# Talking-heads attention with MoE and MLP: softmax scaling moved to GpSimd, a new table of copy costs

## The chip, the cores and the metric

The kernel runs on one core of a Trainium2 chip. The core has a matrix engine (PE, with its weight loads shown apart as PEld), a vector engine (DVE), an activation engine (ACT), GpSimd (POOL) and a queue that issues transfers (SP). Each works through its own list of instructions in order; a semaphore holds an instruction until what it needs is there. The metric is the device time of one launch in microseconds (us). The kernel before took 1386.21 us in the median of three runs (1384.71 to 1386.72).

## The reference

```python
scores = scale * np.matmul(q, k.transpose(0, 1, 3, 2))        # 4 x 12 heads x 448 x 448
scores = np.einsum('bhij,hg->bgij', scores, w_pre)            # heads mixed with each other
scores = scores - np.max(scores, axis=-1, keepdims=True)
attn = np.exp(scores)
attn = attn / (np.sum(attn, axis=-1, keepdims=True) + 1e-09)
attn = np.einsum('bhij,hg->bgij', attn, w_post)               # and mixed again
return np.matmul(attn, v)
```

Its rows (1792 tokens of 768) go through a mixture of eight experts, one per token, and then through an MLP `(h * cos(h)) @ w_out` with `h = x @ w_in`. All is fp32.

## The kernel before

Attention is one long loop in `attention`. The 448 query rows of a batch are cut into four chunks (120, 120, 120, 88 rows). For each chunk and head, `qk` multiplies queries and keys on PE, and the scores go from PSUM to the SBUF tile `S`. To mix heads, a *block* gathers ten query rows of all twelve heads, 120 partitions by 448 (nine rows in the last blocks): `relay` moves them by a transfer from `S` to `x`. There are 180 blocks, and per block these steps follow:

- `premix` (L193): PE multiplies `x` with the mixing matrix `kpre` into `m`; DVE takes the negated row maximum `nm`; ACT makes the exponentials `E` and, by an accumulator, their row sums `sg`.
- `scale` (L206): DVE adds 1e-9 to the sums (`rs`, L210), takes the reciprocal (L211) and multiplies the second mixing matrix `kpost` by it, row by row (`kr`, 120x120, L213). So the softmax is divided by its sums in the weights and not in the exponentials.
- `postmix` (L216), two blocks later: PE multiplies `E` with `kr` into `pa` (four matmuls), and ACT or DVE copies it to `AT`. When a chunk is complete, `av` multiplies with the values (`px`, copied to `xc`), and `rows` turns the result (`pt`, copied to `xr`) for the store.

Between the blocks stand other jobs. In the second half of a batch the keys and queries of the next are turned (`split_k`, `split_q`): ACT rounds the turned keys `tp` to `KH`, DVE takes the rest `KL`, and as each tile needs both halves of its partitions filled, GpSimd copies `KH` (L102) and DVE copies `KL` (L106; in the first batch GpSimd, L104). `narrow64` is the *side conversion*: 64 jobs bring the MLP's weights from eight-byte to four-byte numbers, each with a load `W` (two buffers), a square on ACT (L1294), four DVE operations on `f` (L1299 to L1302; the last three read two SBUF tiles) and a store. `side()` is called once per block and starts a job when its counter has reached one (64 jobs over 170 blocks).

`Balance` deals out the copies that either engine could do. It keeps an account of us for ACT (`act`) and for DVE (`dve`), has a price per copy for each (`a`, `d`), and gives the copy to the engine whose account would be lower; the code adds to the accounts by hand what goes to a fixed engine.

The order in which `attention` is written is not the order on an engine: outside of the stretches marked `manual_schedule` a scheduler of the framework places the instructions by its own costs, so a change in the code moves instructions well beyond its place. The buffers `E` (3), `m` (2), `pa` (2), `kr` (4), `sg` and `rs` (4) bound how far the engines run apart.

Behind attention, `between` and the expert stage start; their first gather, weights and routing follow attention's last blocks.

Of the kernel before, what the change touches and what calls it, by code (L numbers as in the profile page):

```python
# [11 lines left out]
F32 = mybir.dt.float32  # L12
# [6 lines left out]
ALU = mybir.AluOpType  # L19
# [12 lines left out]
class Balance:  # L32
# [4 lines left out]
        self.act = self.dve = 0.0  # L37

    def copy(self, out, in_, n):
        a, d = 0.19 + n * 0.00083, 0.07 + n * 0.00104  # L40
        if self.act + a <= self.dve + d:
            self.act += a
            return self.nc.scalar.copy(out, in_)  # L43
        self.dve += d
        return self.nc.vector.tensor_copy(out, in_)  # L45


def attention(ctx, qctx, tc, q, k, v, w_pre, w_post, wg, xs, lg, ident, nb=4, side=None, route=None):
# [3 lines left out]
    nc = tc.nc  # L52
    B, H, S, D = q.shape
# [10 lines left out]
    bal = Balance(nc)  # L64
# [29 lines left out]
    def split_k1(b, j, i, ps):  # L94

        h = 2 * j + i
        kh = ok.tile([128, S], F32R, tag=f"KH{h}", name=f"KH{b}_{h}")
        kl = ok.tile([128, S], F32R, tag=f"KL{h}", name=f"KL{b}_{h}")
        r, o = HALF[i], HALF[1 - i]
        nc.scalar.copy(kh[r], ps[r, :S])  # L100
        nc.vector.tensor_tensor(kl[r], ps[r, :S], kh[r].bitcast(F32), op=ALU.subtract)
        nc.gpsimd.tensor_scalar(kh[o], kh[r].bitcast(F32), 1.0, 0.0, op0=ALU.mult, op1=ALU.add)  # L102
        if b == 0:
            nc.gpsimd.tensor_scalar(kl[o], kl[r].bitcast(F32), 1.0, 0.0, op0=ALU.mult, op1=ALU.add)  # L104
        else:
            nc.vector.tensor_copy(kl[o], kl[r].bitcast(F32))  # L106
            bal.dve += 0.3
        KH[b, h], KL[b, h] = kh, kl
        bal.act += 0.42
        bal.dve += 0.54  # L110

    def split_q1(b, j, i, ps, cs):

        h = 2 * j + i
        w = slice(112 * cs.start, 112 * cs.stop)
        n = w.stop - w.start
        if cs.start == 0:
            QS[b, h] = ok.tile([128, S], F32R, tag=f"QS{h}", name=f"QS{b}_{h}")
        qs = QS[b, h]
        r, o = HALF[i], HALF[1 - i]  # L120
        nc.scalar.copy(qs[r, w], ps[r, w])
        nc.vector.tensor_tensor(qs[o, w], ps[r, w], qs[r, w].bitcast(F32), op=ALU.subtract)
        bal.act += 0.05 + n * 0.00083
        bal.dve += 0.07 + n * 0.00104

    def split_k(b, j):
        ps = turned(b, j, 0)
# [65 lines left out]
    def premix(n):  # L193
# [5 lines left out]
        e = wk.tile([120, S], F32, tag="E", name=f"E{n}", bufs=3)  # L199
        sg = sm.tile([120, 1], F32, tag="sg", name=f"sg{n}")  # L200
        last["act"] = nc.scalar.activation(e[:M], ps[:M, :S], AF.Exp, bias=nm[:M], scale=1.0, accum_out=sg[:M])  # L201
        bal.act += 0.85
        bal.dve += 0.87
        E[n], SG[n] = e, sg

    def scale(n):  # L206
        X, be, rs, m, M = geom(n)
        sg = SG.pop(n)
        rs_ = sm.tile([120, 1], F32, tag="rs", name=f"rs{n}")
        nc.vector.tensor_scalar_add(rs_[:M], sg[:M], 1e-9)  # L210
        nc.vector.reciprocal(rs_[:M], rs_[:M])  # L211
        kr = sm.tile([120, 120], F32, tag="kr", name=f"kr{n}", bufs=4)
        nc.vector.tensor_scalar_mul(kr[:M], kpost[:M], rs_[:M])  # L213
        KR[n] = kr

    def postmix(n):  # L216
# [149 lines left out]
    for n in range(N + 2):  # L366
        if n < N:
# [6 lines left out]
            if X + 1 < len(chunks):  # L374
# [4 lines left out]
                if nxt[0] == X + 1 and be == nblk - 1:  # L379
                    nxt = [X + 2, 0]  # L380
            premix(n)

            if b + 1 < nb:
                turn = (c - 2) * 12 + be - 2
# [19 lines left out]
                logit_tiles(X - 1)  # L404
        if n >= 2:
            postmix(n - 2)
        if n < N:
            scale(n)
        if side is not None:
            side()  # L410
            bal.dve += 0.6
            bal.act += 0.17
    if side is not None:
        side(True)
    if route is not None:
# [852 lines left out]
def narrow64(ctx, tc, pairs, nblocks, bal=None):  # L1268
# [39 lines left out]
    state = [0, 0.0]  # L1308

    def step(rest=False):  # L1310
        state[1] += len(jobs) / nblocks
        while rest or state[1] >= 1:
            state[1] -= 1
            i = state[0]
            if i >= len(jobs) + 3:
                return
            for s, f in enumerate(stages):
                j = i - (3 - s)
                if 0 <= j < len(jobs):
                    f(j)  # L1320
            state[0] += 1

    return step

# [175 lines left out]
```

## Time and profile before

| | |
|---|---|
| median of three runs | 1386.21 us |
| profiled execution, its own time | 1386.65 us |
| its span | 1384.9 us |
| PE busy | 1325.2 us (96%) |
| DVE busy | 1132.8 us (82%) |
| ACT busy | 866.9 us (63%) |
| POOL busy | 95.5 us (7%) |
| granted PE clock, mean | 0.996 |

The profile is of one execution; the span runs from its first instruction to its last. Busy shares of the whole span mix three stages, attention, experts and MLP, with different limits, so they are read by stretches of time. A wait is the idle time of an engine just before an instruction, put down to what ended it.

### The profile page before, as it was taken

How to read it: one execution, taken by the hardware profiler on the slowest of the kernel's cores; microseconds unless marked ns; L12 is line 12 of the kernel's file. 1: busy time of each engine (PE TensorE's matmuls, PEld its weight loads, DVE VectorE, ACT ScalarE, POOL GpSimd, SP SyncE). 2: the span in 40 equal slices, each digit the busy share in tenths (PEclk: the TensorE clock that was granted, in tenths of full speed). 3: DMA queues.
4: the chain of work that ended last, by engine and by line, in shares of the span. 5: the costliest groups of instructions: out<-in, count | busy, mean ns of one | idle time of the engine just before them, and what ended most of it. 6: DMA issues, size and time to landing. Idle time of an engine off the chain costs nothing.

```text
span 1384.9 us, 24911 instructions
## 1 busy us (share of the span) xinstructions
PE 1325.2 (96%) x8634; PEld 1100.8 (79%) x8634; DVE 1132.8 (82%) x2529; ACT 866.9 (63%) x1598; POOL 95.5 (7%) x127
## 2 busy tenths in 40 slices
PE   6988999899989999899999999999999999999997
PEld 4666777577767777789999999998888888888886
DVE  7889888998997766899999999899877777767663
ACT  7668655765685555788888888776544344444432
POOL 4001000100010000110001000010000010001001
PEclk9999999999999999999999999999999999999999
DMA  7867766676664238147735766256533243224201
GB/s 190 242 198 206 209 205 196 181 220 204 203 188 145 93 114 281 32 140 281 285 137 180 287 241 217 79 184 206 160 114 115 92 137 114 92 92 137 92 23 46
DMA packets 153281, 227.00 MB, mean 164 GB/s; under 512 B 55744, under 2 KB 115392, under 8 KB 153152
## 3 DMA queue, kind: packets, MB, share of 16 engines
q1 hardware_dynamic: 146816, 200.20, 45.9%
q0 software_dynamic: 3744, 18.09, 3.9%
q10 hardware_dynamic: 2592, 7.08, 1.3%
q8 instruction: 70, 1.15, 0.4%
q14 instruction: 59, 0.48, 0.1%
HBM read 217.87 MB, written 31.85 MB: 180 GB/s over the span
## 4 chain that ended last, share of the span: by engine, by line
PE 48%; issue 8%; ACT 0%; DMA 0%; DVE 0%; POOLq 0%; DVEq 0%; ACTq 0%
PE dh L1244 13%; PE op L1194 12%; PE yp L1014 10%; PE h L980 10%; PE ph L1001 1%; PE px L908 1%; PE dpt L1136 1%; DMA out_dram<-o,cout 0%; ACT dhs L1246 0%; ACT woh L819 0%; ACT wih L819 0%; POOLq L1495 0%; ACT gh L1224 0%; PE gspg L757 0%; ACT r L1217 0%
## 5 line engine op out<-in xcount | busy, mean ns | idle before, releaser
L820 DVE TENSOR_TENSOR wl<-r,wh 128x768 fp32r<-128x768 f32 (+1 forms) x246 | 248.9, 1060 | 12.3 <-ACT wh L819 9.4
L819 ACT CAST wh<-r 128x768 fp32r<-128x768 f32 (+1 forms) x246 | 224.0, 931 | 38.6 <-PE h L980 30.3
L223 PEld LDWEIGHTS pa<-kr,E 120*112 120x112 f32 (+1 forms) x1440 | 169.0, 178 | 57.3 <-issue 23.7
L223 PE MATMUL pa<-kr,E 120*112 120x120 f32 (+1 forms) x1440 | 186.2, 271 | 7.2 <-DVE kr L213 3.5
L196 PE MATMUL m<-x,kpre 120*120 120x448 f32 x360 | 167.8, 549 | 10.0 <-ACT E L201 9.1
L201 ACT ACTIVATE E<-m,nm 120x448 f32<-120x448 f32 x180 | 114.0, 633 | 70.5 <-DVE nm L198 51.2
L1244 PE MATMUL dh<-dxh,wih 128*128 128x512 f32 (+1 forms) x384 | 142.6, 371 | 1.2 <-ACT dhs L1246 1.2
L1244 PE MATMUL dh<-dxh,wil 128*128 128x512 f32 (+1 forms) x384 | 140.8, 367 | 0.0
L1244 PE MATMUL dh<-dxl,wih 128*128 128x512 f32 (+1 forms) x384 | 140.6, 366 | 0.0
L819 ACT CAST woh<-wo 128x768 fp32r<-128x768 f32 x64 | 53.2, 833 | 121.3 <-PE op L1194 121.0
L198 DVE TENSOR_REDUCE nm<-m 120x1 f32<-120x448 f32 x180 | 110.7, 615 | 11.5 <-PE m L196 10.5
L1194 PE MATMUL op<-woh,gh 128*128 128x512 f32 x448 | 114.6, 336 | 0.6 <-ACT gh L1224 0.6
L1194 PE MATMUL op<-woh,gl 128*128 128x512 f32 x448 | 114.4, 336 | 0.0
L1194 PE MATMUL op<-wol,gh 128*128 128x512 f32 x448 | 114.4, 336 | 0.0
L170 PE MATMUL s<-KH,QS 128*120 128x448 f32 (+1 forms) x192 | 87.4, 455 | 12.7 <-DVE S L45 4.6
L820 DVE TENSOR_TENSOR wil<-wi,wih 128x768 fp32r<-128x768 f32 x64 | 61.1, 956 | 41.1 <-ACT wih L819 38.6
L1244 PEld LDWEIGHTS dh<-dxh,wih 128*128 128x128 f32 x384 | 72.3, 188 | 14.4 <-ACT dhs L1246 1.7
L1244 PEld LDWEIGHTS dh<-dxh,wil 128*128 128x128 f32 x384 | 72.2, 188 | 13.3
L237 PEld LDWEIGHTS px<-AT,vn 112*64 112x64 f32 x1536 | 75.2, 137 | 8.9 <-ACT AT L43 6.0
L237 PE MATMUL px<-AT,vn 112*64 112x120 f32 (+1 forms) x1536 | 80.9, 261 | 1.3 <-ACT AT L43 1.0
L819 ACT CAST wih<-wi 128x768 fp32r<-128x768 f32 x64 | 53.3, 836 | 45.9 <-PE dh L1244 35.9
L43 ACT COPY S<-s 120x448 f32<-120x448 f32 (+1 forms) x147 | 75.6, 530 | 9.9 <-PE s L171 9.3
(263 smaller groups left out, 2741.0 us busy)
## 6 DMA issues: line engine op xcount, KB each, us to landing
r<-in_moe_w_dram SPq DMA_DIRECT2D x54, 1024.0 KB
r<-in_moe_w_dram SPq DMA_DIRECT2D x72, 768.0 KB
x<-S SPq DMA_DIRECT2D x172, 210.0 KB
wi<-wi SPq DMA_DIRECT2D x32, 768.0 KB
wo<-wo SPq DMA_DIRECT2D x32, 768.0 KB
W<-in_moe_w_in_dram SPq DMA_DIRECT2D x32, 384.0 KB
W<-in_moe_w_out_dram SPq DMA_DIRECT2D x32, 384.0 KB
ys<-y ACTq DMA_DIRECT2D x17, 384.0 KB
```

What stands on the lines that cost most here:

```text
L170: nc.tensor.matmul(ps[:n, :S], QS[b, h][:, i0 : i0 + n], KH[b, h], start=True, stop=False)
L196: nc.tensor.matmul(ps[:M, :S], kpre[:M, :M], XR.pop(n)[:M], start=True, stop=True)
L198: nc.vector.reduce_max(nm[:M], ps[:M, :S], axis=AX.X, negate=True)
L201: last["act"] = nc.scalar.activation(e[:M], ps[:M, :S], AF.Exp, bias=nm[:M], scale=1.0, accum_out=sg[:M])
L223: nc.tensor.matmul(pa[:112, c, :120], e[:M, c * 112 : c * 112 + 112], kr[:M], start=True, stop=True)
L237: nc.tensor.matmul(px[64 * e : 64 * e + 64, pr, :n], VN[b, g // 3][:, g % 3, cc], AT[X][:, cc, g, :n], start=(cc == 0), stop=(cc == 3))
L819: self.latest["A"] = nc.scalar.copy(hi, src).ins
L820: self.latest["V"] = nc.vector.tensor_tensor(lo, src, hi.bitcast(F32), op=ALU.subtract).ins
L980: self.nc.tensor.matmul(hp[n], a[:, k], w[:, n * 512 : n * 512 + 512], start=(k == 0 and i == 0), stop=(k == 5 and i == 2))
L1014: self.nc.tensor.matmul(yp[n][:, :384], a[:, k], w[:, n * 384 : n * 384 + 384], start=(k == 0 and i == 0), stop=(k == 7 and i == 2))
L1194: nc.tensor.matmul(bank[:, to], g[:, t * P : t * P + P], w[:, of], start=first, stop=(f == 15 and i == 2), skip_group_check=(n == 1))
L1244: nc.tensor.matmul(hp[:, :N], w[:, k], x[:, k, :N], start=(k == 0 and i == 0), stop=(k == 5 and i == 2))
```

## The change

Four things change.

1. `scale` is spread out. The added 1e-9 goes to GpSimd and stands in `premix`, right behind the exponentials. The reciprocal stays on DVE but belongs to the block before: it is written behind the next block's `premix`. The multiplication of `kpost` goes to GpSimd.
2. The table of copy prices has other numbers, and so do the amounts that fixed work adds to the two accounts.
3. The copy of `KL` to its other half (batches 2 to 4) is no longer fixed to DVE but dealt out.
4. The conversion's work enters the accounts when a job step is really issued (2.0 us for DVE and 0.56 for ACT), where each block added 0.6 and 0.17.

```diff
     def copy(self, out, in_, n):
-        a, d = 0.19 + n * 0.00083, 0.07 + n * 0.00104
+        a, d = 0.12 + n * 0.00092, 0.06 + n * 0.00124
...
-            nc.vector.tensor_copy(kl[o], kl[r].bitcast(F32))
-            bal.dve += 0.3
+            bal.copy(kl[o], kl[r].bitcast(F32), S)
         KH[b, h], KL[b, h] = kh, kl
-        bal.act += 0.42
-        bal.dve += 0.54
+        bal.act += 0.53
+        bal.dve += 0.62
...
-        bal.act += 0.85
-        bal.dve += 0.87
-        E[n], SG[n] = e, sg
+        bal.act += 0.83
+        bal.dve += 0.77
+
+        rs_ = sm.tile([120, 1], F32, tag="rs", name=f"rs{n}")
+        nc.gpsimd.tensor_scalar(rs_[:M], sg[:M], 1e-9, 0.0, op0=ALU.add, op1=ALU.add)
+        E[n], SG[n] = e, rs_
 
     def scale(n):
         X, be, rs, m, M = geom(n)
-        sg = SG.pop(n)
-        rs_ = sm.tile([120, 1], F32, tag="rs", name=f"rs{n}")
-        nc.vector.tensor_scalar_add(rs_[:M], sg[:M], 1e-9)
+        rs_ = SG.pop(n)
         nc.vector.reciprocal(rs_[:M], rs_[:M])
         kr = sm.tile([120, 120], F32, tag="kr", name=f"kr{n}", bufs=4)
-        nc.vector.tensor_scalar_mul(kr[:M], kpost[:M], rs_[:M])
+        nc.gpsimd.tensor_scalar(kr[:M], kpost[:M], rs_[:M], 0.0, op0=ALU.mult, op1=ALU.add)
...
             premix(n)
+        if 1 <= n <= N:
+            scale(n - 1)
+        if n < N:
...
             postmix(n - 2)
-        if n < N:
-            scale(n)
         if side is not None:
-            side()
-            bal.dve += 0.6
-            bal.act += 0.17
+            done = side()
+            bal.dve += 2.0 * done
+            bal.act += 0.56 * done
```

In `narrow64`, `step` now returns how many job steps it issued. In the lists of the engines 180 adds and 180 multiplications go from DVE to GpSimd. 21 of the 36 `KL` copies and, net, 11 copies of `AT` go from DVE to ACT, and 11 copies of `S` from ACT to DVE; PE and SP have the same instructions as before.

DVE's list around the 22nd block, late in the second chunk, before. `nm` is a block's row maximum, `rs` its sums and their reciprocal, `kr` its scaled weights, `f` the conversion, `AT` a copy:

```order
L198 TENSOR_REDUCE nm_1158<-m_1156 120x1
L210 TENSOR_SCALAR rs_1149<-sg_1135 120x1
L1302 SCALAR_TENSOR_TENSOR f_1845<-sq_1735,f_1845 128x384
L211 RECIPROCAL rs_1149<-rs_1149 120x1
L213 TENSOR_SCALAR kr_1152<-kpost,rs_1149 120x120
L198 TENSOR_REDUCE nm_1188<-m_1186 120x1
L210 TENSOR_SCALAR rs_1169<-sg_1161 120x1
L1299 TENSOR_SCALAR f_1993<-W_1737 128x384
L211 RECIPROCAL rs_1169<-rs_1169 120x1
L1300 SCALAR_TENSOR_TENSOR f_1993<-W_1737,f_1993 128x384
L213 TENSOR_SCALAR kr_1172<-kpost,rs_1169 120x120
L210 TENSOR_SCALAR rs_1199<-sg_1191 120x1
```
The same blocks on DVE now (`nm_1155`, `nm_1185` are `nm_1158`, `nm_1188` of before; the kernel's lines stand one off):

```order
L197 TENSOR_REDUCE nm_1155<-m_1153 120x1
L211 RECIPROCAL rs_1134<-rs_1134 120x1
L1302 SCALAR_TENSOR_TENSOR f_1990<-W_1734,f_1990 128x384
L197 TENSOR_REDUCE nm_1185<-m_1183 120x1
L211 RECIPROCAL rs_1160<-rs_1160 120x1
L1303 SCALAR_TENSOR_TENSOR f_1990<-sq_1847,f_1990 128x384
L211 RECIPROCAL rs_1190<-rs_1190 120x1
L197 TENSOR_REDUCE nm_1205<-m_1203 120x1
L1300 TENSOR_SCALAR f_2088<-W_1849 128x384
L1301 SCALAR_TENSOR_TENSOR f_2088<-W_1849,f_2088 128x384
L211 RECIPROCAL rs_1210<-rs_1210 120x1
```
Where a block had a maximum, an add, a reciprocal and a scaling, it has a maximum and a reciprocal, the reciprocal at times ahead of the next block's maximum and at times behind it, and the conversion's operations stand closer. Over the program the add stood ahead of the next block's maximum in 160 of 178 blocks; now the reciprocal does in 111.

GpSimd's list where the second batch's keys are turned, before: the copies of `KH` to the other half follow each other.

```order
L102 TENSOR_SCALAR KH_0_1305<-KH_0_1305 64x448
L102 TENSOR_SCALAR KH_1_1311<-KH_1_1311 64x448
L102 TENSOR_SCALAR KH_2_1455<-KH_2_1455 64x448
L102 TENSOR_SCALAR KH_3_1461<-KH_3_1461 64x448
L102 TENSOR_SCALAR KH_4_1587<-KH_4_1587 64x448
```
GpSimd's list at the same place now, L205 being the add and L213 the scaling:

```order
L205 TENSOR_SCALAR rs_1273<-sg_1271 120x1
L213 TENSOR_SCALAR kr_1300<-kpost,rs_1273 120x120
L102 TENSOR_SCALAR KH_0_1307<-KH_0_1307 64x448
L205 TENSOR_SCALAR rs_1297<-sg_1295 120x1
L213 TENSOR_SCALAR kr_1409<-kpost,rs_1297 120x120
L102 TENSOR_SCALAR KH_1_1313<-KH_1_1313 64x448
L205 TENSOR_SCALAR rs_1406<-sg_1404 120x1
L102 TENSOR_SCALAR KH_2_1457<-KH_2_1457 64x448
L213 TENSOR_SCALAR kr_1450<-kpost,rs_1406 120x120
L205 TENSOR_SCALAR rs_1447<-sg_1445 120x1
```
Around the `KH` copies stand the adds and scalings of the blocks that run meanwhile, and one `KH` (`KH_2`) stands between the add of a block (`rs_1406`) and the scaling that uses it (`kr_1450`).

ACT's list at the first keys of the same batch, before:

```order
L100 CAST KH_0_1305<-tp_0_0_0_1300 64x448
L201 ACTIVATE E_1297,sg_1298<-m_1293,nm_1295 120x448
L100 CAST KH_1_1311<-tp_0_0_0_1300 64x448
L43 COPY xc_1342<-px_0_1317 128x360
L1294 ACTIVATE sq_2175<-W_2098 128x384
L43 COPY AT_1370<-pa_1371 112x48x10
```
And now:

```order
L100 CAST KH_0_1307<-tp_0_0_0_1302 64x448
L200 ACTIVATE E_1294,sg_1295<-m_1290,nm_1292 120x448
L43 CAST KL_0_1308<-KL_0_1308 64x448
L100 CAST KH_1_1313<-tp_0_0_0_1302 64x448
L1295 ACTIVATE sq_2284<-W_2174 128x384
L43 COPY xc_1344<-px_0_1319 128x360
```
A cast of `KL` stands on ACT behind the block's exponentials and waits for DVE's subtraction (`KL` on L101); the second `KH` cast stands behind it. The square of the conversion has come closer to its neighbours: the list has 50 squares between the 13th and the 109th exponential before, and 57 now.

## Rows read from the trace of the kernel before

**Rows 1.** busy time by stage; us from the span's start, columns in the first line

```profile
core 0: us, PE busy (x) PEld busy (x) DVE busy (x) ACT busy (x) POOL busy (x), PEclk, DMA share, GB/s
...
34.00:553.00 519.00, 485.22 (x4031) 369.78 (x4029) 435.60 (x1388) 327.13 (x788) 23.76 (x38) 1.00 0.63 192
...
600.00:1385.00 785.00, 773.76 (x4203) 679.28 (x4201) 630.74 (x973) 479.40 (x700) 47.86 (x41) 1.00 0.44 151
```

**Rows 2.** busy time of stretches inside the attention stage, same columns

```profile
34.00:425.00 391.00, 358.65 (x2931) 271.85 (x2930) 348.46 (x1058) 256.72 (x611) 22.49 (x36) 1.00 0.68 202
425.00:553.00 128.00, 126.58 (x1101) 97.93 (x1099) 87.14 (x331) 70.42 (x178) 1.27 (x2) 1.00 0.49 161
54.00:90.00 36.00, 31.15 (x249) 23.82 (x248) 30.17 (x91) 20.69 (x51) 0.00 (x0) 1.00 0.72 223
...
286.00:321.00 35.00, 33.22 (x311) 25.25 (x310) 28.83 (x83) 21.54 (x52) 0.00 (x0) 1.00 0.79 230
```

**Rows 3.** waits, 34 to 553 us: who waited <- for whom: us, times, longest

```profile
ACT E L201 <- DVE nm L198: 49.6, 68, 4.1
ACT sq L1294 <- DMA W<-in_moe_w_in_dram: 29.4, 19, 3.2
ACT sq L1294 <- DMA W<-in_moe_w_out_dram: 26.5, 20, 3.0
...
PE pa L223 <- DVE kr L213: 3.5, 9, 1.0
...
PE pa L223 <- DVE rs L210: 2.2, 4, 0.7
```

**Rows 4.** busy time of the scalings (`kr`) alone on DVE, first part

```profile
34.00:425.00 391.00, 35.76 (x128) 1.00 0.68 202
```

**Rows 5.** groups by line and shape: count | busy us, mean ns | idle before

```profile
L43 ACT COPY AT<-pa 112x480 f32<-112x480 f32 x109 | 61.3, 564 | 22.4 <-PE pa L223 21.9
...
L43 ACT COPY S<-s 120x448 f32<-120x448 f32 x108 | 55.4, 532 | 8.2 <-PE s L171 7.8
...
L213 DVE TENSOR_SCALAR kr<-kpost,rs 120x120 f32<-120x120 f32 x172 | 48.0, 279 | 1.7
L45 DVE COPY AT<-pa 112x480 f32<-112x480 f32 x63 | 41.1, 653 | 10.3 <-PE pa L223 9.3 <-issue 0.2
...
L1294 ACT ACTIVATE sq<-W 128x384 f32<-128x384 f32 x64 | 35.8, 559 | 60.4 <-DMA W<-in_moe_w_in_dram 29.4 <-DMA W<-in_moe_w_out_dram 26.5 <-DVE kr L213 1.7
...
L211 DVE RECIPROCAL rs<-rs 120x1 f32<-120x1 f32 x172 | 27.1, 157 | 2.0
...
L210 DVE TENSOR_SCALAR rs<-sg 120x1 f32<-120x1 f32 x172 | 25.5, 148 | 23.5 <-ACT E L201 21.9
...
L45 DVE COPY S<-s 120x448 f32<-120x448 f32 x24 | 14.8, 616 | 0.7 <-PE s L171 0.4
...
L106 DVE CAST KL<-KL 64x448 fp32r<-64x448 f32 x36 | 14.3, 397 | 1.1
...
L447 POOL IOTA part<- 128x1 f32 x1 | 0.1, 127 | 0.0
```

**Rows 6.** single lines: duration ns min/median/max, first and last start us

```profile
L102 POOL TENSOR_SCALAR KH<-KH x48: 557/562/996, 6.7 to 418.6; 64x448 fp32r<-64x448 f32 x48
...
L1300 DVE SCALAR_TENSOR_TENSOR f<-W,f x64: 527/550/896, 30.8 to 423.1; 128x384 int32<-128x384 int32 x64
```

**Rows 7.** timeline, two places: start us, us, engine, line, operation

```profile
118.57 0.53 ACT L100 CAST KH<-tp 64x448 fp32r<-64x448 f32 x1 [0.62 <-PE tp L89]
...
119.18 0.56 POOL L102 TENSOR_SCALAR KH<-KH 64x448 fp32r<-64x448 f32 x1 [6.88 <-PE s L171]
...
261.58 0.56 POOL L102 TENSOR_SCALAR KH<-KH 64x448 fp32r<-64x448 f32 x1 [1.64 <-ACT KH L100]
261.65 0.90 DVE L1300 SCALAR_TENSOR_TENSOR f<-W,f 128x384 int32<-128x384 int32 x1
```

**Rows 8.** sum of three stretches where the next batch is turned, busy us

```profile
sum 145.00, PE 131.43 PEld 101.14 DVE 136.63 ACT 106.36 POOL 22.49; mean PE 43.81 PEld 33.71 DVE 45.54 ACT 35.45 POOL 7.50
```

More of the change, by code (lines that the diff above doesn't have):

```diff
@@ L122, in split_q1 @@
         nc.vector.tensor_tensor(qs[o, w], ps[r, w], qs[r, w].bitcast(F32), op=ALU.subtract)
-        bal.act += 0.05 + n * 0.00083
-        bal.dve += 0.07 + n * 0.00104
+        bal.act += 0.12 + n * 0.00092
+        bal.dve += 0.06 + n * 0.00124
     def split_k(b, j):
@@ L1310, in step @@
     def step(rest=False):
+        done = 0
         state[1] += len(jobs) / nblocks
@@ L1315, in step @@
             if i >= len(jobs) + 3:
-                return
+                break
+            done += 1
             for s, f in enumerate(stages):
@@ L1321, in step @@
             state[0] += 1
+        return done
     return step
```

## The prediction

> **What bounds the kernel now.** I read the busy time by stage first, then by stretches inside the attention stage, then who waited for whom, then the cost of one instruction of each kind. The attention stage ends near 553 us. Behind it, from 600 us on, PE is busy 773.76 of 785 us [rows 1]: the expert and MLP stages run at PE's pace and simply start when attention ends. The change touches attention alone, so its worth is what it moves that end by.
>
> Inside attention there are two parts [rows 2]. From 34 to 425 us the side conversion of the MLP weights runs between the blocks: PE is busy 358.65 of 391 us (91.7%), DVE 348.46 (89.1%), ACT 256.72 (65.7%). From 425 to 553 us, with the conversion done, DVE falls to 87.14 of 128 us (68.1%), and PE rises to 98.9%. So PE's work is the floor, and DVE's load goes with what PE loses above it: 32.4 us idle in the first part, 1.4 in the second. The waits tell the same story: ACT's exponentials waited 49.6 us for DVE's row maxima [rows 3]. A second cause is in the same group: ACT waited 29.4 + 26.5 us for the conversion's loads from DRAM, with copies and exponentials queued behind it. PE itself waited little for the mixing weights, 3.5 us for `kr` and 2.2 us for `rs`, 13 times in all [rows 3].
>
> **The change part by part.**
>
> Scaling and adding leave DVE. In the first part 128 `kr` take 35.76 us [rows 4], and 128 adds of 148 ns [rows 5] take 18.9 us: 54.7 us off DVE. Over the whole stage 21 of the 36 `KL` casts leave too, 21 x 0.397 = 8.3 us. Of the copies, 11 of `AT` go from DVE to ACT and 11 of `S` come back: 11 x 0.653 less, 11 x 0.616 more, 0.4 us net. Together 63.4 us. DVE's 348.5 us become 285.1 us (casts and copies counted as if all stood in this part).
>
> What that gives back is read from two stretches. At a DVE load of 82.4% (28.83 of 35 us, 286 to 321 us) PE was busy 94.9%; at 68.1% it was 98.9% [rows 2]. A DVE load of 285.1 in about 372 us is 76.6%, which lies 0.41 of the way: 96.5% for PE. PE's 358.65 us then take 371.7 us, **19.3 us less**. That is 0.30 us of time for each us taken from DVE. The ends: PE stays at 91.7% (nothing gained), or gets the 98.9% of the second part, 362.6 us (28.4 us gained).
>
> The conversion is packed closer. The order has 57 of the 64 squarings between the 13th and the 109th exponential where it had 50, so one comes every 1.68 blocks instead of 1.92, 14% closer. ACT's wait for loads was 55.9 us over 64, or 0.87 us each. If it grows in proportion, 57 x 0.87 x 0.14 = 7.0 us more stand on ACT, in front of exponentials that free PE's buffers. I count them in full, **7.0 us lost**. The ends are 0 and the difference to the densest stretch: at 54 to 90 us, 8 loads in 36 us, PE was at 86.5% [rows 2], 5.2 points under the mean of the part, which over 300 us is 15.6 us.
>
> ACT gains work: 21 casts at the 559 ns of the squaring, its nearest row that reads SBUF (11.7 us), 11 `AT` copies at 564 ns less 11 `S` copies at 532 ns (0.4 us) [rows 5]. ACT's idle time, 134 us in the first part, covers it; without that cover it is a rival below.
>
> GpSimd's price is not in the trace. The add lies by the smallest row there, an IOTA of one element, 127 ns [rows 5]; the bounds are nothing and the 148 ns of DVE. For the scaling of 120 elements I go between 127 ns for one and the median 562 ns for 448 [rows 6]: 243 ns, bounds 127 and 562. 128 blocks x 0.37 us is 47 us on an engine that was busy 22.5 of 391 us, so it lies beside other work. From ACT's end to GpSimd's start I read 0.08 us (ACT's cast from 118.57 for 0.53 us, GpSimd at 119.18) [rows 7]. The chain from exponential to `kr` is then 0.08 + 0.13 + 0.08 + 0.157 + 0.08 + 0.243 = 0.77 us, against 0.148 + 0.157 + 0.279 = 0.58 on DVE alone without hand-overs. But it passes DVE's queue once, not three times. I count zero; the ends are 0.19 us either way on the 13 occasions PE waited for it, 2.5 us.
>
> New waits, and what stands behind them. The reciprocal waits for GpSimd, and on DVE the next row maximum, copies and conversion work stand behind it. In the old order the add stood ahead of the next block's maximum in 160 of 178 blocks, in the new one the reciprocal does in 111. The added delay, 0.08 + 0.13 us in 111 blocks, is 23 us of DVE's idle time at most, which at 0.30 is 7 us; the 49 blocks where nothing stands in the way any more speak the other way. Zero in the sum, both in the range. On ACT a `KL` cast waits for DVE's subtraction, with the next block's exponential behind it; DVE's freed time covers that, and without it, it is 21 waits of a copy's length, 0.6 us, 13 us on ACT. On GpSimd `kr` stands behind `KH` copies (a rival). SP's order is untouched.
>
> The sum: 1386.65 us (profiled execution, 1.75 us around its span of 1384.9) - 19.3 + 7.0 = 1374.35. The median of the runs is 0.44 us lower, so **1374 us**.
>
> **A rule that speaks against it.** When a `KH` copy on GpSimd began at 261.58, DVE's conversion op that began 0.07 us later took 0.90 us instead of 0.55; behind another that DVE had begun, GpSimd's copy has reached 996 ns instead of 562 [rows 6, 7]. One engine stood still while the other worked. The Trainium skill, "SBUF — State Buffer", section "Who interferes with whom", gives it as a rule: DVE and GpSimd share one pair of ports, which a DVE instruction with two inputs in SBUF and a GpSimd instruction that reads SBUF hold by turns and whole. The trace agrees with it by the durations above. By that rule, moving work from DVE to GpSimd is not free wherever the conversion runs.
>
> **Rivals.**
>
> 1. *The locked port eats the relief (slower).* The 192 two-input conversion ops meet GpSimd's 256 new ones in the first part. If each of the 192 pays what the worst row shows, 0.896 - 0.550 = 0.346 us, DVE gets 66.4 us back, or 20.2 us of time at 0.30: 1386.2 - 12.3 + 20.2 = 1394 us. For it: the rows above. Against it: GpSimd would be busy some 70 of 391 us, 18%, so about 35 of the 192 meet it, and for half of its 0.243 us, 4 us on DVE. It decides from 41 us on, when the mean conversion op exceeds 0.55 + 41/192 = 0.76 us.
>
> 2. *`kr` stands behind `KH` on GpSimd (slower).* GpSimd works in order; in the three stretches where the next batch is turned, 36 `KH` copies now stand among the `add` and `kr`, and each waits for ACT. If each shows on PE with its 562 ns, that is 20.2 us, again 1394 us. For it: the new order below has a `KH` between the add and the `kr` of one block. Against it: PE waited for this chain 13 times in 180 blocks. It decides when PE's waits for `kr` exceed 12.3 + 5.7 = 18 us.
>
> 3. *ACT takes DVE's place where the batch is turned (half the gain).* There ACT is busy 106.36 of 145 us [rows 8]; with 11.7 us of casts and its share of waits for loads, 55.9 x 145/391 = 20.7 us, it is at 138.8, 96%. If nothing is gained there, PE's other 227.2 us of work, at 96.5% in 235.4 instead of 246 us, give 10.6 - 7.0 = 3.6 us: 1383 us. For it: these numbers. Against it: DVE was at 94% in the same stretches, and 54.7 x 145/391 + 8.3 = 28.6 us of that go, 20 points.
>
> 4. *All of it comes back.* PE at 98.9% throughout and no cost from the loads: 1358 us. Against it: the loads' waits are ACT's own and stay.
>
> **How the numbers follow.** The forecast has 0.50, with 1366 to 1381 as its own range (the 7 us of the added waits below, and half of the loads' bounds and of the interpolation above). Rivals 1 and 2 have 0.09 each, rival 3 has 0.20, rival 4 has 0.12. About 0.2%, 2.8 us, is what a measurement of this kernel tells from no change. Faster by more than that: 0.50 + 0.12 + 0.11 of rival 3 = 0.73. Within it: 0.09 of rival 3 and 0.03 of the slower rivals where they only balance = 0.12. Slower: 0.15. The range for 8 in 10 leaves out the lower half of rival 4 and most of rivals 1 and 2: 1359 to 1389 us.
>
> **What would show it.** Right: DVE's busy share up to the conversion's end near 77%, PE's near 96%; ACT's wait for row maxima well under 49.6 us; the last conversion op near 350 us instead of 423 [rows 6], in a stage that ends near 541 us; GpSimd's `kr` near 0.24 us. ACT's wait for the loads near 63 us would confirm the loss, 56 or less would free 7 us, over 75 would make the forecast wrong upward. Conversion ops with a mean over 0.76 us show rival 1, PE waiting 18 us for `kr` rival 2, ACT over 95% busy or waiting where the batch is turned rival 3. The forecast fails if PE's share in the first part does not rise although DVE's falls: then DVE's load was never what held PE.

## The result and the profile after

The changed kernel takes 1402.05 us in the median of four runs (1396.54 to 1405.2), the kernel before 1385.46 us (1382.98 to 1386.72): a ratio of 1.0113, 95% interval 1.0092 to 1.0133. It is slower by some 16 us, where 12 us less were forecast. The profiled execution of after took 1402.46 us, its span is 1400.7 us.

Busy time of the two parts of attention after, with the columns of [rows 2]:

```profile
34.00:425.00 391.00, 355.28 (x2863) 267.27 (x2863) 307.36 (x772) 263.80 (x623) 111.92 (x288) 0.99 0.68 202
425.00:553.00 128.00, 125.12 (x1105) 97.37 (x1102) 65.51 (x215) 71.54 (x178) 27.65 (x94) 1.00 0.41 138
```

DVE's share up to 425 us fell from 89.1% to 78.6%, where 77% were forecast. PE's did not rise: 90.9% where it was 91.7%. GpSimd went from 22.5 to 111.9 us. This pair is the result in short: the engine was relieved, and the work that it was thought to hold up did not notice.

Who waited for whom from 34 to 553 us after (us, times, longest), against [rows 3]:

```profile
...
POOL kr L213 <- DVE rs L211: 67.1, 122, 3.3
DVE rs L211 <- POOL rs L205: 60.5, 82, 3.9
ACT E L200 <- DVE nm L197: 39.7, 48, 2.4
PEld pa L223 <- POOL kr L213: 33.5, 51, 2.3
ACT sq L1295 <- DMA W<-in_moe_w_in_dram: 31.9, 21, 3.8
...
ACT sq L1295 <- DMA W<-in_moe_w_out_dram: 21.0, 19, 2.9
...
PE pa L223 <- POOL kr L213: 8.3, 13, 1.6
```

A new wait stands near the top: DVE's reciprocal for GpSimd's add, 60.5 us, with DVE's other work behind it. For `kr` PE's weight loads (PEld, which overlap its matmuls) waited 33.5 us and its matmuls 8.3 us, where before only the matmuls waited, 3.5 us for `kr` and 2.2 for `rs`. ACT's waits fell a little, for row maxima (39.7 from 49.6) and for loads (52.9 from 55.9).

The costs by line and shape after, as [rows 5]:

```profile
L213 POOL TENSOR_SCALAR kr<-kpost,rs 120x120 f32<-120x120 f32 x172 | 76.0, 442 | 93.5 <-DVE rs L211 67.2 <-PE pa L223 9.8 <-PE s L170 6.8
L205 POOL TENSOR_SCALAR rs<-sg 120x1 f32<-120x1 f32 x172 | 41.9, 244 | 261.2 <-ACT E L200 250.5 <-ACT sq L1295 5.4 <-ACT LT L43 3.3
...
L1301 DVE SCALAR_TENSOR_TENSOR f<-W,f 128x384 int32<-128x384 int32 x64 | 35.8, 559 | 1.0
```

On GpSimd the scaling takes 442 ns, on DVE it took 279; the add 244 instead of 148. The conversion's operations on DVE take what they took.

Where the 15.8 us between the two spans arise is read from three places. The last mixing matmul of `m` (duration ns min/median/max, first to last start), before and then after:

```profile
L196 PE MATMUL m<-x,kpre x360: 537/539/1073, 28.4 to 551.5; 120*120 120x448 f32 x172, 108*108 108x448 f32 x8
```
and
```profile
L195 PE MATMUL m<-x,kpre x360: 537/539/954, 27.6 to 559.1; 120*120 120x448 f32 x172, 108*108 108x448 f32 x8
```

So 7.6 us are lost inside the blocks. PE's clock is not the reason: up to the last `m` it was granted at half (1.2 instead of 2.4 GHz) for 6.8 us before and for 10.2 us after, and in e1 below, with 6.8 us of it, the last `m` starts at the same 559.1 us. The rest belongs to two gathers behind them, which GpSimd issues. Its timeline, the first gather before:

```profile
498.84 1.08 POOL L900 DMA_INDIRECT xg<-xs,ids  x1 [79.55 <-DVE rs L211]
```
and after:
```profile
560.75 1.10 POOL L901 DMA_INDIRECT xg<-xs,ids  x1 [0.79 <-DVE u L576]
561.90 0.37 POOL L213 TENSOR_SCALAR kr<-kpost,rs 108x120 f32<-108x120 f32 x1
562.35 0.22 POOL L205 TENSOR_SCALAR rs<-sg 108x1 f32<-108x1 f32 x1
562.93 0.37 POOL L213 TENSOR_SCALAR kr<-kpost,rs 108x120 f32<-108x120 f32 x1 [0.37 <-DVE rs L211]
```

The gather now stands in GpSimd's list among the last blocks' scalings, 62 us later, and takes 1.10 us in front of one of them. The first expert matmul starts at 570.4 us instead of 560.4: 2.4 us more. PE's first matmuls on the gathered rows (`px`), before:

```profile
555.70 0.82 PE L908 MATMUL px<-ident,xg 128*128 128x128 f32 x6
```
and after, with PE's wait ahead of them:
```profile
562.32 0.87 PE L223 MATMUL pa<-kr,E 108*112 108x120 f32 x6 [1.79 <-POOL kr L213]
...
564.69 1.49 PE L909 MATMUL px<-ident,xg 128*128 128x128 f32 x6
```
and the busy times of a stretch around them (the last three columns are the granted clock, the DMA share and GB/s):
```profile
563.80:567.20 3.40, 3.40 (x29) 3.07 (x29) 0.74 (x1) 2.56 (x4) 0.00 (x0) 0.50 0.59 159
```

PE stood idle for 1.79 us until the scaling behind the gather was done, and soon after its clock was at half, 1.2 GHz, for 3.4 us. e1 has the same place in the list and the same wait (1.80 us) without the fall of the clock, and there only half of the 2.4 us are lost.

The second gather before, with DVE's operations beside it and PE's wait for it:

```profile
575.45 7.22 DVE L820 TENSOR_TENSOR wl<-r,wh 128x768 fp32r<-128x768 f32 x7
575.80 3.18 POOL L900 DMA_INDIRECT xg<-xs,ids  x1 [75.69 <-DVE ids L685]
...
581.72 0.87 PE L908 MATMUL px<-ident,xg 128*128 128x128 f32 x6 [1.70 <-DMA xg<-xs,ids]
```
and after:
```profile
585.90 7.23 DVE L821 TENSOR_TENSOR wl<-r,wh 128x768 fp32r<-128x768 f32 x7
586.26 7.79 POOL L901 DMA_INDIRECT xg<-xs,ids  x1 [22.84 <-DVE ids L686]
...
596.83 1.54 PE L909 MATMUL px<-ident,xg 128*128 128x128 f32 x6 [6.38 <-DMA xg<-xs,ids]
```

The same gather at the same place beside the same seven subtractions took 7.79 us instead of 3.18, and PE waited 4.7 us longer for it. Its clock was at half from 594.5 to 601.3 us, so that the six matmuls behind the wait took 1.54 us instead of 0.87. Some 6 us arise here in the profiled run; the runs of after lie 8.7 us apart.

### The profile page after: what moved, and what is told of

Read it like the earlier page. It is cut to its first block, busy times and chain, and to the rows that moved or that the text cites. A ratio compares the mean times of both kernels' runs of the same rounds, so it can differ in the third digit from the quotient of the medians.

```text
span 1400.7 us, 25281 instructions
## 1 busy us (share of the span) xinstructions
PE 1332.2 (95%) x8634; PEld 1105.4 (79%) x8634; DVE 1076.1 (77%) x2142; ACT 880.8 (63%) x1625; POOL 220.6 (16%) x487
## 4 chain that ended last, share of the span: by engine, by line
PE 46%; issue 8%; DVE 1%; DMA 1%; ACT 1%; POOLq 0%; DVEq 0%; ACTq 0%
PE dh L1245 12%; PE op L1195 11%; PE yp L1015 10%; PE h L981 10%; PE ph L1002 1%; PE px L909 1%; PE dpt L1137 0%; DMA wi<-wi 0%; DMA out_dram<-o,cout 0%; ACT wih L820 0%; DVE wil L821 0%; DVE wol L821 0%; ACT dhs L1247 0%; ACT woh L820 0%; DVE r L1216 0%
## 5 line engine op out<-in xcount | busy, mean ns | idle before, releaser
L223 PE MATMUL pa<-kr,E 120*112 120x120 f32 (+1 forms) x1440 | 189.5, 273 | 11.0 <-POOL kr L213 10.1
L213 POOL TENSOR_SCALAR kr<-kpost,rs 120x120 f32<-120x120 f32 x180 | 79.3, 441 | 97.0 <-DVE rs L211 69.4
L205 POOL TENSOR_SCALAR rs<-sg 120x1 f32<-120x1 f32 x180 | 43.8, 243 | 269.4 <-ACT E L200 258.4
L43 ACT COPY AT<-pa 112x480 f32<-112x480 f32 (+1 forms) x126 | 71.0, 563 | 21.7 <-PE pa L223 21.1
```

The lines of the kernel that those rows point to most:

```text
L223: nc.tensor.matmul(pa[:112, c, :120], e[:M, c * 112 : c * 112 + 112], kr[:M], start=True, stop=True)
```

## The experiments

All runs in one table. "Last m" is the last start of the matmuls of `m`, read as above (the expectations give the last block's first, 0.3 to 0.4 us earlier).

| run | median us (lowest to highest, runs) | ratio to before, interval | last m us |
|---|---|---|---|
| e1 scaling moved alone | 1396.81 (1394.63 to 1408.14, 6) | 1.0089 [1.0059, 1.0119] | 559.1 |
| e2 table alone | 1387.05 (1382.96 to 1389.61, 12) | 0.9998 [0.9984, 1.0011] | 552.1 |
| e3 last 24 blocks on DVE | 1397.08 (1392.6 to 1397.29, 6) | 1.0065 [1.0048, 1.0083] | 559.5 |
| e4 no scaling | 1380.5 (1376.74 to 1383.52, 7) | 0.9949 [0.9932, 0.9966] | 546.6 |
| e5 after, paced | 1387.77 (1384.39 to 1396.51, 11) | 1.001 [0.9994, 1.0025] | 552.8 |
| e6 before, paced | 1386.96 (1380.33 to 1390.12, 12) | 0.9993 [0.9976, 1.001] | 551.5 |
| e7 no scaling, paced | 1389.4 (1382.09 to 1392.18, 8) | 1.0017 [1.0, 1.0034] | 556.8 |
| e8 add back on DVE | 1392.85 (1388.78 to 1397.58, 6) | 1.0052 [1.0033, 1.0072] | 555.9 |
| e9 before, conversion behind | 1530.28, one run | | 514.3 |
| e10 after, conversion behind | 1536.28, one run | | 523.4 |
| e11 no scaling, conversion behind | 1518.67, one run | | 508.5 |
| e12 DVE waits for the gather | 1399.62 (1398.49 to 1404.0, 4) | 1.0112 [1.0086, 1.0138] | 558.8 |
| e13 no loads | 1362.34, one run | | 527.4 |
| e14 last step on GpSimd | 1400.94 (1399.97 to 1403.75, 4) | 1.0116 [1.0094, 1.0139] | 566.1 |
| e15 two of four steps | 1388.43, one run | | 554.6 |
| e16 e3 + e5 + e12 | 1387.24 (1383.23 to 1393.06, 10) | 1.0007 [0.9992, 1.0023] | 551.8 |
| e17 loads nobody reads | 1398.1, one run | | 561.3 |
| e18 loads from GpSimd | 1431.76 (1429.67 to 1436.65, 4) | 1.033 [1.0285, 1.0374] | 589.4 |

A "last m" is read from one execution of each kernel. After, e1, e3 and e12 lie at 558.8 to 559.5 us, before, e2 and e6 at 551.5 to 552.1, so the 7.6 us are clear; a difference of some 3 us between two single executions is not. In e9 to e11 the conversion runs alone behind attention, so there the time of the whole tells nothing.

**Which part carries the loss: e1, e2, e8.** e1 is the changed kernel with the table, the amounts and the `KL` copies of before; e2 is the other half. e8 puts the add back on DVE:

```diff
-        nc.gpsimd.tensor_scalar(rs_[:M], sg[:M], 1e-9, 0.0, op0=ALU.add, op1=ALU.add)
-        E[n], SG[n] = e, rs_
+        E[n], SG[n] = e, sg
...
+        nc.vector.tensor_scalar_add(rs_[:M], sg[:M], 1e-9)
         nc.vector.reciprocal(rs_[:M], rs_[:M])
```

> Only the move of the scaling: add and multiplication on GpSimd, reciprocal a block later; prices, KL copies and accounts as before. Theory A (the hand-overs to and from GpSimd hold DVE and PE up, and its gathers stand behind the scaling): slower by 10 to 16 us, as with the whole change, with GpSimd's add near 0.24 us, the scaling near 0.44 us and DVE idle some 60 us in front of reciprocals. Theory B (the new table is at fault: denser conversion, more copies on ACT): within 3 us of before or up to 10 us faster.

> Only the new prices, the dealt-out KL copies and the conversion's accounts; the scaling on DVE as before. Theory A: no slower than before, -8 to +2 us, first gather issued near 499 us as before. Theory B: slower by 5 us or more, ACT waiting more than 56 us for the conversion's loads.

> The whole change, but the add is back on DVE in front of the reciprocal; only the scaling is on GpSimd, so DVE waits for ACT alone. Theory A: a third to a half of the loss in the attention stage goes (3 to 5 us under the whole change, DVE's wait for GpSimd gone). Theory E: within 2 us of the whole change.

The table is worth nothing; the scaling's move loses its 7.6 us in the blocks with either table. With the add on DVE 3.2 of them come back (559.1 to 555.9) and the reciprocal's wait goes from 67 to 2 us over the kernel; the median is 9 us lower than after's, and part of that belongs to the second gather (3.22 us long in e8's profile). The scaling alone on GpSimd still costs 0.5%. So the move is what loses; by which way is another question. The chain itself did not get longer: from the end of a block's exponentials to the end of its scaling it took 1.62 us before and 1.35 after, in the median of the 180 blocks.

**What is DVE's load worth? e4, and the pacing of e5 to e7.** e4 takes add, reciprocal and scaling out altogether (`KR[n] = kpost`; the softmax isn't divided by its sums): 180 x (148 + 157 + 279) ns, or 105 us off DVE by the durations. Pacing ties each conversion step behind its block's activation, on before, on after and on e4:

```diff
-        side()
+        with tc.issue_after(last["act"].ins):
+            side()
```

> The kernel before, leaving out the added 1e-9, the reciprocal and the scaling of the mixing weights: PE takes the unscaled mixing matrix, so the output is not divided by the row sums. This takes some 104 us off DVE and the whole chain from the exponentials to kr. The prediction's step (0.30 us of time for each us off DVE where the conversion runs, 73 of the 104 us): faster by about 20 us. Theory D (DVE's load was not what held PE): faster by less than 8 us.

> The whole change, with the conversion held to the pace at which its jobs are written: each job's square stands on ACT behind the exponential of the block it is written at, one per 2.7 blocks over the whole stage, where it was one per 1.7 blocks over the first 108. Theory E (the conversion was packed closer and ate what DVE was relieved of): faster than the whole change by 8 us or more (under 1394 us) and no longer slower than before. Theory A (the hand-overs between DVE and GpSimd hold DVE's and PE's lists up, whatever the conversion does): stays 5 us or more above the paced kernel before, DVE still waiting some 60 us in front of reciprocals.

> The kernel before with the same pace. Theory E: faster than before by 5 us or more, as ACT no longer waits some 56 us for the conversion's loads. Theory A says nothing of it; if the loads never mattered, within 3 us of before.

> The kernel without scaling (it leaves out the added 1e-9, the reciprocal and the scaling of the mixing weights) with the same pace: the relief of DVE without the closer conversion. Theory E: the relief that e4 did not show appears, 15 us or more under before. Theory D (DVE's load never held PE): not more than 3 us under the paced kernel before.

e4's busy time in the first part:

```profile
34.00:425.00 391.00, 360.04 (x2945) 277.75 (x2945) 309.80 (x680) 257.97 (x618) 21.10 (x36) 0.99 0.68 203
```

DVE is at 79.2%, PE at 92.1%, the stage ends 4.9 us earlier: 0.05 us for each us taken off DVE, not 0.30. But the conversion ran ahead here too (its last operation on DVE starts at 358 us instead of 425), so its loads came closer. With the pace they keep their places. The first part of e6:

```profile
34.00:425.00 391.00, 365.34 (x2977) 279.46 (x2975) 335.89 (x1016) 256.07 (x612) 22.05 (x36) 0.99 0.60 182
```
and of e7:
```profile
34.00:425.00 391.00, 358.61 (x2934) 279.17 (x2934) 285.74 (x615) 248.71 (x598) 21.52 (x36) 0.98 0.59 179
```

DVE falls from 85.9% to 73.1% at nearly the same DMA share, and PE does not rise; the last `m` starts 5.3 us later. Nothing is left of the gain. Pacing takes ACT's wait for the loads away (0.1 us in e5, none in e6) and gives before nothing; but in e6 ACT waits longer for row maxima instead (74.6 us over the kernel, 51.2 before), so what the loads' wait alone was worth stays open. Pacing also makes the changed kernel as fast as before, with the last `m` at 552.8 us, although DVE's reciprocals wait 66.6 us for GpSimd there and PE's weight loads and matmuls 35.4 and 8.5 us for `kr`, as much as in after. So these waits by themselves do not make the loss; why the pace takes it away is not shown.

**Without the conversion: e9 to e11.** Before, after and e4 with the conversion behind attention; the amounts in the accounts stay:

```diff
     def step(rest=False):
         state[1] += len(jobs) / nblocks
+        if not rest:
+            n = int(state[1])
+            state[1] -= n
+            return n
...
-        side(True)
+        with tc.issue_after(last["act"].ins):
+            side(True)
```

> The kernel before with the side conversion moved behind attention (two jobs' first three DVE operations stay ahead of it), its amounts in the accounts kept, so that the copies are dealt out as before. The place to read is the start of the last block's mixing matmul (551.2 us in the kernel before), not the time of the whole, which grows by the conversion at the end. Theory (PE in the first part is held by what the conversion puts on the engines in order, its loads and stores above all): the last block starts 20 to 30 us earlier, at 521 to 531 us, PE above 97% from 34 us on. Rival (PE is held by the chain of attention itself, relays and row maxima): less than 10 us earlier.

> The changed kernel with the conversion moved behind attention in the same way. Theory (the loss inside the blocks is the hand-over between GpSimd and DVE together with the conversion's operations that stand on DVE): without the conversion the last block starts within 3 us of the kernel before without its conversion. Rival (the longer chain from the exponentials to the scaled weights costs PE by itself): it starts 5 to 8 us later than there, as it does with the conversion (558.7 against 551.2).

> The kernel before without added 1e-9, reciprocal and scaling (that part of the softmax is left out), the conversion moved behind attention. Theory (DVE's load is not what holds PE): within 2 us of the kernel before without its conversion, though DVE has some 100 us less. Rival (what the forecast went by, 0.30 us for each us off DVE): some 20 us or more earlier, or as far as PE's own work lets it.

The conversion costs attention 37.2 us (551.5 to 514.3), more than I expected. My theory on e10 fell: without it the changed kernel is not level but 9.1 us behind (523.4). The move by itself costs some 0.05 us in each of 180 blocks, no single wait takes it, and the chain from exponentials to scaling takes 1.19 us in the median in both, so the way it costs is open. Leaving out the scaling is worth 5.8 us here, for the same 105 us off DVE. e10's costs of the moved operations:

```profile
L213 POOL TENSOR_SCALAR kr<-kpost,rs 120x120 f32<-120x120 f32 x172 | 63.2, 368 | 75.9 <-DVE rs L211 57.1 <-PE pa L223 5.4 <-PE s L170 4.6
L205 POOL TENSOR_SCALAR rs<-sg 120x1 f32<-120x1 f32 x172 | 37.0, 215 | 269.0 <-ACT E L200 263.3 <-ACT LT L43 3.3 <-ACT AT L43 1.3
```

Without the conversion's two-input operations beside them the scalings take 368 ns instead of 442 and the adds 215 instead of 244. In after itself the 62 scalings that ran beside such an operation took 561 ns in the mean, the 110 others between 34 and 553 us 372.

**What of the conversion holds PE: e13, e15, then e17.** e13 makes two of the 64 loads, e15 leaves out two of the four DVE operations (in both the converted weights are not the reference's), e17 makes all loads into a tile that nobody reads:

```diff
 e13, def load(i):
+        if i > 1:
+            W[i] = WW[i % 2]
+            return
 e15, def bits(i):
-        V.scalar_tensor_tensor(f, w[:, :, 0], 29, f, op0=ALU.logical_shift_right, op1=ALU.bitwise_or)
-        V.scalar_tensor_tensor(f, w[:, :, 1], -0x40000000, f, op0=ALU.bitwise_and, op1=ALU.bitwise_or)
 e17, def load(i):
+        t = wk.tile([P, C, 2], I32, tag="W" if i else "W0", name=f"W{i}", bufs=1)
+        nc.sync.dma_start(out=t, in_=...)
+        W[i] = WW.setdefault(0, t)
```

> The kernel before, where only the first two of the conversion's 64 loads are made and all jobs work on these two tiles (so the converted weights are those of two pieces; squares, the four DVE operations and the stores stay). Place to read: the start of the last block's mixing matmul, 551.2 us before and 513.9 without the conversion, 37.3 us. Theory L (the loads' waits in ACT's list, 55.9 us, hold PE): the last block starts at 530 us or earlier. Rival D (the conversion's own operations among the blocks' hold it): 545 us or later. In between, the share goes by the place.

> The kernel before with the second and third of the conversion's four DVE operations left out (the converted weights are then not those of the reference); loads, squares and stores stay. 70 us less on DVE. Rival D: the last block starts 15 to 19 us earlier than 551.2. Theory L: less than 5 us earlier. What the scaling gave (104 us off DVE for 4.9 us here, in the run without scaling) would make it 3 us.

> The kernel before, where all 64 loads of the conversion are made, at the places they had in SP's list, but land in one tile that no engine reads; every job works on the first load's tile (the converted weights are those of one piece). So the traffic stays and the waits for it and for the buffers go. Place to read: the start of the last block's mixing matmul, 551.2 us before, 527.0 without the loads. Theory W (the waits: ACT's squares for the loads, SP's loads for a free buffer with the relays behind them): it starts near 527, 532 at most. Rival T (the traffic of 24 MB slows the transfers between the blocks): 545 us or later.

Busy time to 425 us in e13:

```profile
34.00:425.00 391.00, 375.21 (x3141) 289.19 (x3140) 361.48 (x1104) 271.39 (x644) 22.25 (x36) 1.00 0.47 150
```
and in e15:
```profile
34.00:425.00 391.00, 356.60 (x2902) 271.35 (x2901) 297.48 (x925) 253.69 (x605) 20.59 (x36) 0.99 0.68 202
```

In e13 DVE is busier than before (92.5%) and PE rises to 96.0%; in e15 DVE falls to 76.1% and PE stays at 91.2%. Taking the loads away ends the blocks 24.1 us earlier (one execution), taking 70 us of durations off DVE ends them no earlier. In e15 the loads did not stay where they were: the conversion's last operation starts at 316 us instead of 425, so a gain could have been lost to closer loads. That DVE's load alone is worth next to nothing rests on e7 and e11. The loads are 24 of the 37 us; the other 13 belong to squares, DVE operations and stores, which no run takes apart.

By which way the loads act is open; taking ACT's wait away gave nothing (e6). e17 was to separate traffic from waits, but with one tile each load waits in SP's list for the one before. SP's waits up to 425 us in e17:

```profile
SPq L1290 <- DMA W<-in_moe_w_out_dram: 35.7, 20, 4.6
SPq L1290 <- DMA W<-in_moe_w_in_dram: 30.4, 19, 3.0
```

So 66.1 us of waiting stand in front of the relays, and its 561.3 us can come from that or from the traffic, or in part from PE's clock, which was at half for 30.7 us up to there (6.8 before). In the records of the transfers a relay (120 packets of 1792 bytes) takes 3.17 us in the mean from its issue to its last packet's end before, 3.35 in e17, 2.63 without the loads, 2.51 without the conversion: beside the loads the relays take longer. But PE waited for a relay 0.7 us in all, so the link from there to PE is not shown.

**Two tries to use it: e14, e18.** e14 makes the conversion's last step on GpSimd (`sq` compared, then multiplied with `f`); e18 issues the loads from GpSimd (`nc.gpsimd.dma_start`).

> The kernel before with the last of the conversion's four DVE operations (0.55 us x 64 = 35 us) as two on GpSimd. If PE follows the conversion's time on DVE (37.3 us for 141 us of it, 0.26 us each), the last block starts 9 us earlier and the kernel takes about 1377 us. If PE follows only the waits, or GpSimd's hold on the shared port costs what DVE saves: within 3 us of the kernel before. Slower than 1389 us would mean that the conversion's own chain, now longer, holds ACT and DVE.

> The kernel before with the conversion's loads issued by GpSimd instead of SP, so that a load that waits for its buffer (39.9 us of SP's time up to 425 us) no longer stands ahead of the relays. Theory S (SP's order is a good part of what the loads cost): the last block starts 10 us or more earlier than 551.2 and the kernel takes 1376 us or less. Rival (the squares' wait on ACT is what costs, or the loads take longer from GpSimd): within 4 us of the kernel before, or slower.

Both lose. e14's two operations:

```profile
L1302 POOL TENSOR_SCALAR sq<-sq 128x384 f32<-128x384 f32 x64 | 98.6, 1541 | 68.2 <-ACT sq L1294 58.9 <-DVE f L1301 1.9 <-DVE l L580 1.8
L1303 POOL TENSOR_TENSOR f<-sq,f 128x384 f32<-128x384 f32 x64 | 65.0, 1017 | 94.8 <-issue 44.9 <-DVE rs L211 22.2 <-DVE f L1301 20.0
```

They take 2.56 us where DVE took 0.55, and SP waited 47.0 us for load buffers and 25.6 for finished pieces up to 425 us (39.9 and 14.4 before); what of it costs the 14.6 us no run takes apart. In e18 ACT's squares waited 84.8 us for the loads (55.9 before); so it can't tell what the place in SP's list costs.

**The gathers: e3, e12, e16.** e3 keeps add and scaling of the last 24 blocks on DVE. e12 makes DVE's next operations wait until the second gather has landed. e16 has both and the pacing of e5.

```diff
 e3, both operations:
-        nc.gpsimd.tensor_scalar(
+        (nc.gpsimd if n < len(blocks) - 24 else nc.vector).tensor_scalar(
 e12, behind self.gather(1):
+        seen = self.early.tile([P, 1], F32, name="seen")
+        self.nc.vector.tensor_copy(seen, self.G[1][:, :1])
```

> The whole change, but the last 24 of the 180 blocks add and scale on DVE again, so that GpSimd's list is free for the first gather of the expert stage. Theory C (2 to 3 us are lost because that gather stands among the last scalings, and some 6 us because the second gather is held up by DVE): first gather issued near 500 us instead of 561, no wait of PE for kr at the end; the total 2 to 3 us under the whole change (about 1399 us), and 8 to 9 us under it if the second gather also takes 3 us instead of 8. Without theory C: as the whole change, 1402 us.

> The changed kernel with one more DVE operation: behind the issue of the second gather, DVE copies one column of what it brings, so DVE's run of two-input subtractions starts only when the gather has landed. Theory (the gather takes 7.79 us where DVE's run of seven subtractions shuts GpSimd out, 3.18 where it does not): the gather takes about 3.2 us in the profile, and all runs lie close together near 1397 to 1400 us, where the changed kernel's had 1396.5 in one run and 1401.6 to 1405.2 in three. Rival (the transfer itself, not DVE, makes it long): a gather of 7.8 us in the profile or a spread of 5 us or more over the runs.

> The changed kernel with three things together: add and scaling of the last 24 blocks on DVE (so the first gather does not stand behind GpSimd's scalings), the conversion paced behind each block's activation, and DVE waiting for the second gather. If the pieces add up: last block at 552, first expert matmul at 562, no long second gather, about 1385 us, the same as the kernel before. Rival (something else of the change still costs): 1390 us or more.

In e3 the first gather is issued at 506.6 us and the first expert matmul follows the last `m` by 8.8 us, as before. Its second gather took 3.19 us, and its span is 1392.6 us, 7.7 more than before: the loss of the blocks alone. e12's timeline at the second gather:

```profile
585.98 1.05 POOL L901 DMA_INDIRECT xg<-xs,ids  x1 [22.84 <-DVE ids L686]
589.76 0.15 DVE L1059 COPY seen<-xg 128x1 f32<-128x1 f32 x1 [4.05 <-DMA xg<-xs,ids]
589.83 7.22 DVE L821 TENSOR_TENSOR wl<-r,wh 128x768 fp32r<-128x768 f32 x7
```

With DVE standing still the gather takes 1.05 us, not 3.18 or 7.79: it is DVE's run that makes it long. What decides between 3.18 and 7.79 stays open. e12's median is only 2.4 us under after's, and the half of my expectation on the spread failed: one run is still at 1404.0, so the gather is not all that sets the runs of after apart. e16 takes the pieces away together and is level with before, but e5, which leaves both gathers as they are in after, is level too (1387.24 and 1387.77 us). In e5 two runs of 11 stand apart at 1396.4 and 1396.5 us, the others at 1389.6 or less; the profiled one is of the two, and its second gather took 7.79 us. So the sum of the three pieces holds for the profiled execution of after; how often the gather is long the medians do not tell. No version with the scaling on GpSimd beats the kernel before.

## Why the prediction was wrong, step by step

- **The failed step: "That is 0.30 us of time for each us taken from DVE."** It was read from two stretches and the mean of the first part [rows 2]. Between the first part and the second, the conversion stops: with it go its DVE operations, but also its loads, and the DMA share in the same rows falls from 0.68 to 0.49. DVE's load and the loads changed together, and I gave all of PE's gain to DVE. With the loads in their places (e7) or away (e11), 105 us off DVE moved the last `m` 5.3 us later and 5.8 us earlier; without the loads (e13) it came 24.1 us earlier with DVE busier than before. So the 19.3 us of the sum were next to nothing, and of the 37 us that the conversion costs two thirds go with its loads. (The stretch at 286 to 321 us fits neither alone: DMA 0.79, PE 94.9%.) The text's last sentence had named this as what would make it fail.
- **DVE's relief** had the right sign and two thirds of the size: 348.46 to 307.36 us to 425 us, 41.1 us where 63.4 were forecast. The sum took durations off a busy time. The durations of DVE's records there add up to 409.1 us in a stretch of 391, and to 344.1 after; they overlap, so 65 us of durations were 41 us of busy time. The conversion's last operation came at 367 us instead of 425 (forecast 350). The conversion ran ahead; PE did not.
- **The loads' 7.0 us** were looked for in the wrong place: ACT's wait fell by 3.0 us. What rose was SP's wait for a free load buffer, with relays behind it. SP's waits to 425 us, before:

```profile
SPq L1290 <- DVE f L1301: 39.9, 24, 3.2
```
and after:
```profile
SPq L1291 <- DVE f L1302: 62.9, 34, 6.0
```
  That is 23 us more of waiting in SP's list. "SP's order is untouched" was no answer for what its instructions wait for; what these 23 us cost PE no run shows alone.
- **GpSimd's price**: the scaling at 442 ns lies within its bounds (127 to 562) but far from the 243 taken; the add at 244 lies above its upper bound of 148. DVE's duration was no bound for another engine.
- **The chain and the new waits, counted at zero**: the move they belong to costs 7.6 us to the last `m` (e1), of which the add's part is 3.2 in one execution (e8). The chain is not the way, it became shorter (1.35 us for 1.62), and waits as long as these cost only 1.3 us with the pace (e5), so the way stays open. A hand-over took 0.10 us (GpSimd idle 0.37 us around a reciprocal of 0.16), near the 0.08 assumed. The bound on DVE's wait was 23 us; it is 60.5, in 82 waits of 0.74 us: DVE often stood there long before the add had begun, which the bound (delay by the add's own duration) did not allow for.
- **Left out: the gathers.** GpSimd's list was searched for `KH`, not for what follows attention in it. Two gathers there, with PE's fallen clock behind them, cost some 8 us of the profiled 15.8.
- **Rivals.** Rival 1's sign (conversion operations over 0.76 us) did not show: 0.56 us. The port works the other way, GpSimd is the one that stands: 442 against 368 ns in e10, and in after 561 ns beside a conversion operation against 372. The rule cited, of the Trainium skill, "SBUF — State Buffer", section "Who interferes with whom", has the loser of the pair wait; the trace agrees and shows which one loses here. Rival 2's number (PE waiting over 18 us for `kr`) was passed with 41.8 us only if the weight loads' 33.5 us are counted; the matmuls waited 8.3. Its mechanism is not what costs: 9 of the 180 scalings follow a `KH` copy in GpSimd's list, and 7 of these waited on for something else. That its 1394 us were nearer than mine is luck. Rival 3 did not decide: in the three stretches of [rows 8] PE's busy time is 132.62 us against 131.43, with ACT at 111.61. Rival 4 is out.

## What to carry to other kernels

A slope between an engine's load and the time holds only if nothing else changes between the stretches it is read from; look along the same rows for a second column that moves (here DMA), and before you count on the relief, leave the work out once and see whether the time notices. An idle engine is not a free one: a short operation split over two in-order engines puts a wait into the lists of both, and whatever follows it there, down to the next stage's first transfers, moves too. Durations that overlap can't be taken one for one off a busy time.

## What the runs showed of the hardware that was not expected

- An indirect gather on GpSimd took 1.05 us with DVE standing still, and 3.18 or 7.79 us beside the same run of seven two-input subtractions of 1 us each on DVE; in the slow case it ended 0.9 us after the run. The same section ("Who interferes with whom") of the Trainium skill's "SBUF — State Buffer" infers that an operation of this kind (`tensor_tensor`) leaves descriptor generation alone; here the gather as a whole was held up. Which of its parts stood still, no run shows.
- One element for each partition on GpSimd costs 215 ns and 120 elements 368 ns without the conversion beside them (e10), 384 elements in two tensors 1017 ns beside it (e14), where DVE took 148, 279 and some 555 (the last with a comparison in it).
- The 64 loads of 384 KB cost attention 24 us (e13), yet without ACT's wait for them it ended no earlier (e6): by which wait they cost it, no run shows.
